# Moving key and softmax-weight transposes from TensorE to the SP DMA queue in an attention + FFT-gate kernel

## The chip, the cores and the metric

The kernel runs on one core of one Trainium2 chip. The metric is device time of one launch in microseconds (us); lower is better. A profile is one launch seen by the hardware profiler; its span is about 2 us shorter than the launch. Executions come in a fast and, at times, a slower state with a lower granted TensorE clock; verdicts use fast runs. Engines: PE is TensorE, PEld its weight loads, DVE VectorE, ACT ScalarE, POOL GpSimd, SP the SyncE queue that issues DMAs (SPq in the tables). An instruction that issues a DMA holds SP for a time; the next one in the queue can only start after it. A DMA lands when its data has arrived.

## The reference, cut to what matters

```python
# q, k, v: (8, 8, 576, 64); p: (8, 8, 32, 64)
p_packed = sm_attn(p, k, v)              # 32 packed queries read 576 keys
out = sm_attn(q, p_packed, p_packed)     # 576 queries read the 32 packed ones
x = out.transpose(0, 2, 1, 3).reshape(8, 576, 512)
proj = x @ w_proj                        # three blocks x1, x2, x3
y = x1 * irfft(rfft(x2) * rfft(filter)) * x3
return y @ w_out
```

## The kernel before: what the change and the argument touch

All is in fp16 on TensorE with fp32 sums. The kernel treats batches 0 to 7 as a pipeline of four stages: `front` (both attentions), `turn` (projection, first part of the spectrum, transposed softmax weights), `middle` (spectrum and gate) and `back` (inverse and output product). A helper records every operation and then plans the order of each engine with a cost model of its own, which takes 60 ns for issuing a DMA on SP and keeps the best of eight plans. All operations therefore carry one source line, L440, and any edit can move instructions far from it.

Three operands must be turned so that the contracted index lies on the partitions: queries `qT`, keys `kT`, and the normalised softmax weights `a2t`. Queries of batches 4 to 7 are turned by DMA on SP already:

```python
TURNED = 4
...
if b >= TURNED:                                   # in load(b)
    nc.sync.dma_start_transpose(qT.rearrange("p h i c -> p (h i) c"),
                                qn.rearrange("p h x -> p (h x)"))
```

Keys and weights are turned on PE, into a PSUM tile that DVE or ACT copies to SBUF:

```python
def k_turn(g):                                    # in front(b), four groups a batch
    tp = pst(f"kTp_b{b}", [P, 2, 3, KP], FP16)
    for hh in range(2):
        for ii in range(3):
            nc.tensor.transpose(tp[:, hh, ii, :], kn[:, 2 * g + hh, ts(ii, P)], ident[0:KP, 0:KP])
    ...                                           # copy on DVE or ACT
...
for t in range(2):                                # in turn(b)
    tp = pst(f"a2tp_b{b}", [P, S], FP16)
    nc.tensor.transpose(tp[:, ds(COL0[4] - 64 * t, P)], a2c, ident[:])
    for i in range(4):
        to = tp[:, ds(COL0[i], P)] if i != 2 else ...   # column order of the spectrum
        nc.tensor.transpose(to, a2n[:, i, ts(t, P)], ident[:])
    nc.vector.tensor_copy(out=a2t[:, t, :], in_=tp[:])
```

SP issues in its own order, and the stores of the outputs go through it too, from five buffers `os`.

The softmax here doesn't subtract the row's maximum and nothing guards it: scores larger than these inputs give would overflow.

## Time and profile before

| before | value |
|---|---|
| time, median of 3 runs | 201.28 us (200.71 to 203.0) |
| span of the profiled run | 198.3 us at a mean clock of 0.992 |
| PE busy from 131.4 to 190 us | 57.97 of 58.60 us |
| PE transposes: keys, weights | 192 of 96x96, 80 of 128x128 |

PE is the bound: the prediction below shows the busy lines, the chain and the stretches. A stretch line is read as its window in us, its length, then busy time with the number of instructions for PE, PEld, DVE, ACT and POOL, then the granted clock (1.00 is full), the DMA share and GB/s.

### The profile page before, as it was taken

Reading aid. Unit: us, or ns where it says so; the run is one execution under the profiler, and the core shown is the slowest. Engines: PE = TensorE matmul, PEld = TensorE weight load, DVE = VectorE, ACT = ScalarE, POOL = GpSimd, SP = SyncE. Lnnn points to the kernel's source line nnn. Section 1 sums busy time; section 2 is a strip of 40 time slices with the busy share of each in tenths; the row PEclk is TensorE's granted clock in tenths of the full one; section 3 lists DMA queues with packets and bytes.
Section 4 is the critical chain, followed back from the end, with each engine's and each line's share of the span. In section 5 each row is a group of like instructions: output and inputs, shape, how many; then the busy total and the mean of one; then the engine's idle time right before and its main releaser. Section 6 shows DMA issues by size and latency. Waiting matters only on the chain.

```text
span 198.3 us, 5799 instructions
## 1 busy us (share of the span) xinstructions
PE 184.8 (93%) x2413; PEld 114.7 (58%) x2413; DVE 142.2 (72%) x268; ACT 126.4 (64%) x265; POOL 133.5 (67%) x108
## 2 busy tenths in 40 slices
PE   4879989989999999999999999999999999999990
PEld 2226555666765775766665666565756465664630
DVE  4246857998369699966896699668966996798610
ACT  2247567597879978758874878478758556416050
POOL 7404578878566699989966996299529985963100
PEclk9999999999999999999999999999999999999996
DMA  5999999999999999889999999943013103503235
GB/s 136 270 269 197 205 207 198 196 199 195 202 217 268 189 201 179 165 116 244 263 173 156 112 126 201 172 130 85 3 55 107 56 0 118 143 10 132 81 126 141
DMA packets 44843, 30.96 MB, mean 156 GB/s; under 512 B 16336, under 2 KB 39376, under 8 KB 44816
## 3 DMA queue, kind: packets, MB, share of 16 engines
q0 software_dynamic: 29312, 16.52, 60.9%
q1 hardware_dynamic: 14784, 13.34, 28.9%
q10 hardware_dynamic: 720, 0.72, 1.2%
q8 instruction: 19, 0.31, 0.6%
q14 instruction: 8, 0.07, 0.1%
HBM read 35.55 MB, written 9.44 MB: 227 GB/s over the span
## 4 chain that ended last, share of the span: by engine, by line
PE 73%; DVE 8%; DMA 7%; POOL 4%; ACT 3%; issue 1%; ACTq 0%; DVEq 0%; POOLq 0%
PE x_b L440 28%; PE o_b L440 14%; PE f_b L440 7%; DMA kn_b<-in_k_dram 7%; PE fp_b L440 5%; PE s_b L440 4%; DVE tt_b L440 3%; PE kTp_b L440 3%; PE pv_b L440 3%; PE qp_b L440 3%; PE hp L440 2%; DVE zs_b L440 2%; PE a2tp_b L440 2%; PE qTp_b L440 1%; POOL gm_b L440 1%; POOL fa_b L440 1%
## 5 line engine op out<-in xcount | busy, mean ns | idle before, releaser
L440 POOL TENSOR_TENSOR gm_b<-tt_b,tt_b 128x512 f16<-128x512 f32 (+1 forms) x28 | 39.3, 1431 | 5.8 <-DVE tt_b L440 5.3
L440 DVE TENSOR_TENSOR tt_b<-f_b,h 128x1024 f32<-128x1024 f32 x32 | 38.7, 1214 | 4.7 <-PE f_b L440 4.1
L440 PE MATMUL x_b<-a2t_b,qm_b 128*128 128x512 f16 (+1 forms) x256 | 40.9, 286 | 0.2
L440 PE MATMUL x_b<-ac,gm_b 128*128 128x64 f16 (+3 forms) x312 | 36.0, 252 | 0.1
L440 ACT ACTIVATE os_b<-o_b 128x512 f32<-128x512 f32 x36 | 21.4, 597 | 21.8 <-PE o_b L440 21.8
L440 PE MATMUL o_b<-wout,y_b 128*128 128x512 f16 x128 | 33.4, 379 | 0.0
L440 ACT CAST qm_b<-qp_b 128x512 f16<-128x512 f32 x48 | 26.6, 590 | 10.6 <-PE qp_b L440 10.5
L440 POOL TENSOR_TENSOR tt_b<-tt_b,tt_b 128x1024 f32<-128x1024 f32 x12 | 28.3, 2360 | 5.0 <-DVE tt_b L440 4.9
L440 DVE TENSOR_TENSOR w_b<-x1s_b,x_b 128x512 f32<-128x512 f32 (+1 forms) x40 | 24.6, 627 | 8.9 <-ACT x1s_b L440 8.7
L440 ACT COPY x1s_b<-x_b 128x512 f32<-128x512 f32 (+1 forms) x40 | 21.9, 547 | 11.1 <-PE x_b L440 7.7
L440 PEld LDWEIGHTS <-gm_b 128*128 128x128 f16 x312 | 22.3, 98 | 8.8 <-POOL gm_b L440 2.6
L440 POOL TENSOR_TENSOR fa_b<-ez_b 128x512 f16<-128x512 f32 x14 | 17.6, 1273 | 14.2 <-ACT ez_b L440 14.2
L440 PE MATMUL f_b<-qm_b,fa_b 128*128 128x512 f16 x80 | 24.1, 379 | 0.4 <-DVE tt_b L440 0.2
L440 ACT ACTIVATE e_b<-s_b 96x384 f16<-96x384 f32 (+1 forms) x48 | 23.5, 533 | 1.1 <-PE s_b L440 1.0
L440 DVE SCALAR_TENSOR_TENSOR y_b<-w_b,x_b 128x512 f16<-128x512 f32 x32 | 20.6, 681 | 3.9 <-PE x_b L440 3.7
L440 PEld LDWEIGHTS <-a_b 128*128 128x128 f16 x240 | 15.9, 98 | 8.5 <-POOL a_b L440 1.2
L440 PEld LDWEIGHTS <-qm_b 128*128 128x128 f16 x256 | 15.7, 98 | 8.6 <-issue 1.1
L440 POOL TENSOR_TENSOR a_b<-e_b,zr_b 128x1152 f16<-128x1152 f16 (+2 forms) x10 | 17.3, 1735 | 3.5 <-ACT qm_b L440 2.4
L440 PEld LDWEIGHTS <-y_b 128*128 128x128 f16 x128 | 11.9, 98 | 11.5 <-DVE y_b L440 0.6
L440 PE MATMUL kTp_b<-ident,kn_b 96*128 96x96 f16 x192 | 13.0, 205 | 0.9 <-DVE tt_b L440 0.5
L440 PEld LDWEIGHTS <-kn_b 96*128 96x128 f16 x192 | 11.0, 97 | 4.7 <-issue 2.0
L440 ACT COPY ez_b<-fp_b 128x512 f32<-128x512 f32 x16 | 9.4, 586 | 3.7 <-PE fp_b L440 3.4
(78 smaller groups left out, 280.4 us busy)
## 6 DMA issues: line engine op xcount, KB each, us to landing
out_dram<-os_b SPq DMA_DIRECT2D x24, 256.0 KB, 2.7
kn_b<-in_k_dram POOLq DMA_DIRECT2D x8, 576.0 KB, 13.1
vn_b<-in_v_dram POOLq DMA_DIRECT2D x8, 576.0 KB, 14.8
qn_b<-in_q_dram POOLq DMA_DIRECT2D x8, 512.0 KB, 15.1
out_dram<-os_b SPq DMA_DIRECT2D x16, 128.0 KB, 2.4
wp<-in_moe_w_proj_dram POOLq DMA_DIRECT2D x3, 512.0 KB, 18.5
filt<-in_moe_filter_fft_dram SPq DMA_DIRECT2D x4, 256.0 KB, 6.6
out_dram<-os_b SPq DMA_DIRECT2D x16, 64.0 KB, 1.9
```

Of the source, the lines that this page charges most:

```text
L440: ins = op.call(*op.args, **op.kw).ins
```

## The change

The intent is to take PE time out of the stretches where PE is full. Keys of batches 6 and 7 (four DMAs of 144 KB a batch) and softmax weights of batches 5 to 7 (twelve DMAs a batch, six of 128 rows and 128 columns and six of 64 rows) are turned on SP. Queries of batches 4 to 7 stay as they were.

```diff
--- before.py
+++ after.py
@@ -506,7 +506,8 @@
 
     pflat = p.rearrange("b h j d -> (b h j) d").rearrange("(b t r) d -> r b t d", t=2, r=P)
 
-    TURNED = 4
+
+    TURNED, TURNED_K, TURNED_A = 4, 6, 5
 
 
     loaded, small = {}, {}
@@ -664,20 +665,27 @@
                 nc.vector.tensor_copy(out=qTm[:, :, u, c].rearrange("p g (e r) -> p g e r", e=2),
                                       in_=tp[:, :, c].rearrange("p g (r e) -> p g e r", e=2))
 
-        k_turn(0)
-        yield 260
+        for g in range(4) if b >= TURNED_K else ():
+            nc.sync.dma_start_transpose(kTr[g][:, 0:6 * KP].rearrange("p (x r) -> p x r", r=KP),
+                                        kn[:, 2 * g:2 * g + 2, :].rearrange("p h x -> p (h x)"))
+        if b < TURNED_K:
+            k_turn(0)
+            yield 260
         pack()
         yield 230
-        k_turn(1)
-        yield 260
+        if b < TURNED_K:
+            k_turn(1)
+            yield 260
         score1(0)
         yield 270
-        k_turn(2)
-        yield 260
+        if b < TURNED_K:
+            k_turn(2)
+            yield 260
         score1(1)
         yield 270
-        k_turn(3)
-        yield 260
+        if b < TURNED_K:
+            k_turn(3)
+            yield 260
         score1(2)
         yield 270
         if b < TURNED:
@@ -807,7 +815,12 @@
         nc.scalar.copy(out=fa[:, :, 512:640].rearrange("p t (u f) -> p t u f", u=2),
                        in_=fp[:].unsqueeze(2).broadcast_to([P, 2, 2, 64]))
         yield 300
-        for t in range(2):
+        for t in range(2) if b >= TURNED_A else ():
+            for i in range(4):
+                for r, c in ((slice(0, P), COL0[i]),) if i != 2 else ((slice(0, 64), 320), (slice(64, P), MAIN)):
+                    nc.sync.dma_start_transpose(a2t[:, t, c:c + r.stop - r.start], a2n[r, i, ts(t, P)])
+            nc.sync.dma_start_transpose(a2t[:, t, ds(COL0[4], 64)], a2c[64 * t:64 * t + 64, :])
+        for t in range(2) if b < TURNED_A else ():
             tp = pst(f"a2tp_b{b}", [P, S], FP16)
 
             nc.tensor.transpose(tp[:, ds(COL0[4] - 64 * t, P)], a2c, ident[:])
```

## The prediction

> **What bounds the kernel now.** I read the page first, then the busy times in stretches that follow the kernel's own rhythm, then the waits, and then the timeline around the work that the change takes away. The page says that TensorE (PE) is busy almost throughout at a granted clock that the slices print as 9 in all but the last one, and that no other engine is close:
>
> ```profile
> PE 184.8 (93%) x2413; PEld 114.7 (58%) x2413; DVE 142.2 (72%) x268; ACT 126.4 (64%) x265; POOL 133.5 (67%) x108
> ...
> PE 73%; DVE 8%; DMA 7%; POOL 4%; ACT 3%; issue 1%; ACTq 0%; DVEq 0%; POOLq 0%
> ```
>
> One batch passes every 20.7 us in the steady part: the first key transposes of successive batches start at 114.7 and 135.3 us. Cut into such periods, and the last two stretches without attention work, the columns are PE, weight loads, DVE, ACT, POOL busy, granted clock, DMA share, GB/s:
>
> ```profile
> 90.00:110.70 20.70, 20.55 (x292) 13.08 (x289) 16.07 (x29) 14.99 (x34) 17.00 (x14) 1.00 1.24 203
> 110.70:131.40 20.70, 20.61 (x297) 13.27 (x295) 16.54 (x30) 15.31 (x34) 15.23 (x10) 1.00 1.11 149
> 131.40:152.10 20.70, 20.23 (x286) 12.96 (x284) 16.16 (x30) 14.74 (x33) 14.22 (x10) 1.00 0.23 68
> 152.10:170.00 17.90, 17.74 (x165) 10.05 (x163) 14.94 (x24) 10.83 (x22) 14.70 (x10) 1.00 0.23 69
> 170.00:188.00 18.00, 18.00 (x146) 10.61 (x144) 14.05 (x21) 5.76 (x11) 9.09 (x6) 1.00 0.29 89
> ```
>
> PE is full in each (20.55 of 20.70, 18.00 of 18.00), DVE has 4 us to spare in a period and POOL 3 to 6. So PE's own stream sets the time from about 80 us to 188 us, and PE time taken out there should come off the end. The DMA column matters too: the engines are full (above 1.0, because packets of two queues overlap) until the last loads land at about 123 us, and nearly idle afterwards.
>
> **What the skill says.** (1) "VectorE: DVE Perf Modes", section "The three transpose paths", gives 390 ns for a 128x128 transpose on TensorE and 1309 ns by DMA. In this trace PE pipelines them: six key transposes hold the stream 0.31 us and five weight transposes 0.25 us (below), so 390 ns would overstate the gain seven times. (2) "DMA: Bandwidth & Descriptors", section "Anatomy of one DMA", puts about 2 us of fixed cost on each transfer, mostly the receipt. The trace agrees: the 64 KB output stores late in the run land 1.7 us after issue (median), the 256 KB ones 2.1. (3) The same page, "Issuing engines are not separate DMA queues", says that all queues share the same 16 engines and interleave. The trace shows how hard this bites: the four query transposes already there move 512 KB each, and their issue and landing depend on what else runs:
>
> ```profile
> L440 SPq DMA_TRANSPOSE qT_b<-qn_b x4: 1937/5840/10869, 73.7 to 112.8; - x4
> ...
> DMA to landing us min/median/max: 4.3/10.9/18.1
> ...
> 79.41 1.94 SPq L440 DMA_TRANSPOSE qT_b<-qn_b  x1
> ...
> 102.86 6.79 SPq L440 DMA_TRANSPOSE qT_b<-qn_b  x1
> ...
> 112.78 10.87 SPq L440 DMA_TRANSPOSE qT_b<-qn_b  x1
> ```
>
> Alone on the engines (79.4 us) one held SP for 1.94 us and landed in 4.3; beside the loads of the next batch it held SP for 6.8 and 10.9 us, and the one of 102.86 landed 18.1 us later. (4) "Advanced Engine Details and Errata", section "X-Bar Transpose (TRN2)", calls them as fast as ordinary DMAs; that holds here for the lone case at best.
>
> **The change, part by part.** Removed from PE: for batches 6 and 7 four groups of six 96x96 key transposes, for batches 5 to 7 two groups of five weight transposes. The weight-load stream shows what each group costs, as the distance to the next load behind it:
>
> ```profile
> 141.25 0.37 PEld L440 LDWEIGHTS <-kn_b 96*128 96x128 f16 x6
> 141.56 0.36 PEld L440 LDWEIGHTS <-qm_b 128*128 128x128 f16 x3
> ...
> 151.43 0.29 PEld L440 LDWEIGHTS <-a_b 128*128 128x128 f16 x5
> 151.68 0.15 PEld L440 LDWEIGHTS <-y_b 128*128 128x128 f16 x2
> ```
>
> Keys: 4 x 0.31 = 1.25 us a batch, two batches 2.5 us. Weights: 2 x about 0.27 = 0.54 us a batch, three batches 1.6 us. Sum 4.1 us of PE, all after about 114 us, where PE is full. Also removed: eight copies of kT (0.45 us on DVE, 0.64 on ACT, four each) and six of a2t (0.45 us on DVE), 7.1 us of two engines that don't bound, so worth nothing directly; and their PSUM tiles.
>
> Added on SP: 8 key pieces of 144 KB, and 36 small weight transposes (12 a batch). SP is in order, the built program gives it eight completion semaphores in turn, and each issue waits for the transfer eight before it. For a small one I estimate 0.45 to 0.5 us of SP: a plain store held it 0.33 to 0.59, and the lone 512 KB transpose, sixteen blocks, 1.94, so about 0.1 per block on top. Twelve take 6 us, plus some 2.3 us to land: 8 to 8.5 us from weights to transposed weights.
>
> Is each in time? In the instruction order of the changed program the weights of batch 6 are ready, by the old trace's times, some 15 us before their first gate, and those of batch 7 are ready at 160.3 (end of the POOL normalisation) with the first gate at about 171: 10.7 us once the PE transposes are out of the way, against 8.4. Both are hidden, the second with 2 us to spare. Those of batch 5 sit behind the query and key transposes of batch 7 on SP, and come out about where PE wants them (I get 135 us for both), so 0 to 1 us of wait. Keys of batch 7 fall after 123 us, with idle DMA engines, and have several us to spare.
>
> The keys of batch 6 are the weak place. On SP they come straight behind the query transpose of batch 6, between 97 and 120 us, where the loads of batch 7 run. The old trace moved the 2048 packets of that query transpose at roughly 170 a us beside the loads and near 1000 alone. Queries and keys of batch 6 are now 2048 + 2304 packets. The changed order loads the queries of batch 6 earlier (the value load of batch 5 moves ahead), so SP can start near 96 rather than 102.86; at a mixed rate the last piece lands between 114 and 124 us. PE wants the first piece at about 116.5 and the fourth at about 119. Taking the landing as even over 113 to 125, the mean wait is 6/12 x 3 = 1.5 us, with up to 5 possible.
>
> One more loss: key transposes now fill PE while it waits for the gated spectra from POOL:
>
> ```profile
> PEld L440 <- POOL gm_b L440: 2.2, 6, 0.5
> ```
>
> That is over 114 to 160 us. With filler gone the wait may grow by some tenths; I set 0.3 us for this and for batch 5's weights together.
>
> Sum: 201.28 - 4.1 + 1.5 + 0.3 = 199.0 us.
>
> **Rivals.** (a) Everything is hidden and the whole 4.1 us comes off: 197.2. For it: PE is at 18.00 of 18.00 in the tail, batch 7 has slack, DMA is nearly idle after 123. Against it: the mixed DMA rates just shown. (b) The keys of batch 6 come 4 to 5 us late. PE runs in order, so this undoes the gain, and delays what SP holds behind them: 200.5 to 202. For it: the 18.1 us landing. Against it: the earlier query load. (c) SP becomes the bound through output stores queued behind transposes, as the five output buffers fill and ACT, then PSUM, then PE stop. In the changed order at most four or five outputs stand behind a block of transposes, just what the buffers hold, so I give this little; it would cost 2 to 4 us, 201 to 203. (d) The kernel plans its order anew, and the plan differs from the start of the program, where nothing was edited (other order of the filter products, 32 fillers for 35). That moves the time by perhaps 1 us either way and can't be foreseen from the profile.
>
> **Range and chances.** The full gain is 2.0% of 201.28, so over 2% faster needs nearly all of it kept and some luck with the new plan or with the keys: 0.20. Slower by over 2% (205.3) needs (b) and (c) together: 0.07. Rest 0.73. Range 196.4 (full gain and 0.8 us of luck) to 202.0 (rival b).
>
> **What would show it.** Right: in the changed profile PE's key transposes count 144 instead of 192 and the weight ones 50 instead of 80, PE's waits from 110 us on are mainly for kT of batch 6 (1 to 2 us in all) and little for a2t; the small transposes hold SP about 0.5 us each; the period between batches falls from 20.7 to about 19. Wrong: a wait of over 3 us at the score products of batch 6; a2t waits of over 1 us for batch 6 or 7 (then the small transposes cost SP much more than 0.5 us); ACT waiting for output buffers; or a difference that is already there at 80 us, which would be the new plan and not the transposes.

## The result, and the profile after

The changed kernel takes 219.22 us (median of 4 runs, 215.86 to 221.16); the kernel before took 201.0 us (199.9 to 203.0) beside it. Ratios here are the mean time of one kernel's fast runs over that of the other's in the same rounds, so not quite the ratio of the quoted medians: 1.083, with a 95% interval of 1.064 to 1.102. The change makes the kernel 8% slower, and the prediction of 199.0 us with a range up to 202.0 is wrong.

The page of the profile after, its busy line, its clock line (one digit for each of 40 slices, 9 is full speed) and the chain of work that ended last:

```profile
PE 186.7 (87%) x2332; PEld 112.4 (53%) x2332; DVE 139.1 (65%) x258; ACT 124.5 (58%) x261; POOL 133.4 (62%) x108
...
PEclk9999999999999999999999999975799889999999
...
PE 53%; SPq 20%; DMA 12%; DVE 6%; ACT 3%; issue 2%; POOL 2%; ACTq 0%; DVEq 0%
```

PE has 81 instructions fewer than before (2332 for 2413: 78 transposes and 3 of the `spin` matmuls that fill idle time) and is yet busy for longer; its clock sinks in slices 27 to 29, 32 and 33. The SP queue, which had no part in the chain before, now makes up 20% of it. The three late stretches, same windows as in the prediction but for the last, which ends at 190 (there PE was busy for all of 170 to 190 us before):

```profile
131.40:152.10 20.70, 13.14 (x123) 7.23 (x120) 7.46 (x12) 9.72 (x21) 11.86 (x8) 0.75 0.37 61
152.10:170.00 17.90, 16.07 (x214) 9.10 (x213) 13.24 (x22) 11.70 (x24) 12.44 (x9) 0.97 0.23 55
170.00:190.00 20.00, 18.17 (x138) 10.19 (x136) 12.87 (x19) 7.91 (x15) 12.71 (x8) 0.94 0.26 69
```

PE is idle for 20.70 - 13.14 = 7.6 us of the first, where it had been idle for 0.5, and for 11.2 us of all three. The DMA engines are mostly idle too (0.23 to 0.37), so it isn't bandwidth. What does SP do meanwhile? Its timeline (start, us, instruction, count):

```profile
121.14 4.90 SPq L440 DMA_TRANSPOSE qT_b<-qn_b  x1
126.14 0.52 SPq L440 DMA_DIRECT2D out_dram<-os_b  x1
126.78 6.04 SPq L440 DMA_TRANSPOSE kT<-kn_b  x4
132.90 16.08 SPq L440 DMA_TRANSPOSE a2t_b<-a_b  x12
149.09 4.34 SPq L440 DMA_DIRECT2D out_dram<-os_b  x8
153.53 16.36 SPq L440 DMA_TRANSPOSE a2t_b<-a_b  x12
169.99 3.11 SPq L440 DMA_DIRECT2D out_dram<-os_b  x6
173.21 15.65 SPq L440 DMA_TRANSPOSE a2t_b<-a_b  x12
```

From 132.90 to 188.9 us SP is free for 0.11 us at most between two instructions, but for one gap of 0.46 us. Twelve small transposes keep it for 15.7 to 16.4 us, not 6. A store holds it for 4.34 / 8 = 0.54 us. The group of the weight transposes (minimum, median and maximum hold in ns) and its landing:

```profile
L440 SPq DMA_TRANSPOSE a2t_b<-a_b x36: 1093/1226/1828, 132.9 to 187.6; - x36
...
DMA to landing us min/median/max: 2.2/2.4/3.9
```

The median hold is 1.23 us. From the start of its first transpose to the landing of its last a batch needs 16.8 to 17.5 us (the landing counts from the issue, so the last hold is in it), where the prediction counted 8 to 8.5 and had 10.7. What PE then waits for, in its timeline (idle time before the piece in brackets):

```profile
121.11 0.26 PE L440 MATMUL s_b<-pk,kT 128*128 128x64 f16 x3 [1.63 <-DMA kT<-kn_b]
123.15 0.35 PE L440 MATMUL s_b<-pk,kT 128*128 128x64 f16 x6 [0.82 <-DMA kT<-kn_b]
...
140.99 0.38 PE L440 MATMUL x_b<-a2t_b,qm_b 128*128 128x512 f16 x1 [1.50 <-DMA a2t_b<-a_b]
...
147.71 1.44 PE L440 MATMUL x_b<-a2t_b,qm_b 128*128 128x512 f16 x3 [5.86 <-DMA a2t_b<-a_b]
...
187.63 0.81 PE L440 MATMUL x_b<-a2t_b,qm_b 128*128 128x512 f16 x3 [1.83 <-DMA a2t_b<-a_b]
```

The list of waits sums them up (us, times, longest):

```profile
PE x_b L440 <- DMA a2t_b<-a_b: 9.2, 3, 5.9
...
PEld L440 <- DMA kT<-kn_b: 3.0, 3, 1.8
PE s_b L440 <- DMA kT<-kn_b: 2.4, 2, 1.6
```

PEld runs beside PE, so the last two rows are largely one wait, of about 3 us. A fourth wait of PE for the weights stands under `issue`: 1.83 us up to 168.58, when a weight transpose of batch 6 had just landed (168.49).

The clock adds to it. Its records give half speed from 141.78 to 152.02 us, a stretch that begins with the 5.86 us wait (141.86 us), just after two shorter ones (0.20 and 1.50 us), and from 169.08 to 172.50, after the wait that ended at 168.58. PE is busy for 4.38 and 3.42 us of these; at full speed about half of that would have done (an estimate), so they cost some 3.9 us.

Where the time comes from is easiest to see at fixed points of the program. The kernel makes 36 output products; every fourth of them, from the first on, is a fixed point, nine in all. The table gives their starts in the profiled runs (us):

| | 1st | 4th | 5th | 6th | 7th | 8th | 9th |
|---|---|---|---|---|---|---|---|
| before | 50.8 | 111.3 | 131.0 | 149.0 | 165.8 | 178.8 | 189.3 |
| after | 52.3 | 113.5 | 134.9 | 161.5 | 180.3 | 194.7 | 205.3 |
| difference | +1.5 | +2.2 | +3.9 | +12.5 | +14.5 | +15.9 | +16.0 |

The working: +2.2 us by the 4th point, which is there at the 2nd already (83.5 and 85.6 us), while SP issues the first moved transpose at 107.44 us; +1.7 to the 5th (the wait of 3.0 for keys of batch 6, less the 1.25 of PE work taken away); then 11.2 - 0.6 = 10.6 us more PE idle time, + 3.9 for the clock, - 2.9 for the other PE work taken away (1.6 for weights, 1.25 for keys of batch 7). After 190 us PE has no idle time up to the 9th point in either run. The sum is 15.5 us; the spans differ by 214.0 - 198.3 = 15.7.

### The profile page after: what moved, and what is told of

It is laid out like the page before. It is cut to its first block, busy times and chain, and to the rows that moved or that the text cites.

```text
span 214.0 us, 5700 instructions
## 1 busy us (share of the span) xinstructions
PE 186.7 (87%) x2332; PEld 112.4 (53%) x2332; DVE 139.1 (65%) x258; ACT 124.5 (58%) x261; POOL 133.4 (62%) x108
## 4 chain that ended last, share of the span: by engine, by line
PE 53%; SPq 20%; DMA 12%; DVE 6%; ACT 3%; issue 2%; POOL 2%; ACTq 0%; DVEq 0%
SPq L440 20%; PE x_b L440 18%; PE o_b L440 8%; DMA kT<-kn_b 6%; PE hp L440 4%; PE f_b L440 4%; PE fp_b L440 4%; PE s_b L440 4%; DMA filt<-in_moe_filter_fft_dram 3%; DVE tt_b L440 2%; DMA a2t_b<-a_b 2%; PE pv_b L440 2%; PE qp_b L440 2%; PE kTp_b L440 2%; PE qTp_b L440 2%
## 5 line engine op out<-in xcount | busy, mean ns | idle before, releaser
L440 PE MATMUL x_b<-a2t_b,qm_b 128*128 128x512 f16 (+1 forms) x256 | 42.2, 291 | 11.4 <-DMA a2t_b<-a_b 9.2
L440 PE MATMUL x_b<-ac,gm_b 128*128 128x64 f16 (+3 forms) x312 | 38.2, 260 | 0.4 <-ACT qm_b L440 0.4
L440 POOL TENSOR_TENSOR tt_b<-tt_b,tt_b 128x1024 f32<-128x1024 f32 x12 | 28.3, 2358 | 16.1 <-DVE rz_b L440 15.1
L440 PE MATMUL o_b<-wout,y_b 128*128 128x512 f16 x128 | 33.9, 379 | 0.0
L440 PEld LDWEIGHTS <-gm_b 128*128 128x128 f16 x312 | 23.3, 100 | 10.6 <-issue 2.3
L440 POOL TENSOR_TENSOR fa_b<-ez_b 128x512 f16<-128x512 f32 x14 | 17.6, 1271 | 13.6 <-ACT ez_b L440 13.6
L440 PEld LDWEIGHTS <-a_b 128*128 128x128 f16 x210 | 13.9, 98 | 8.4 <-POOL a_b L440 1.5
L440 PE MATMUL s_b<-pk,kT 128*128 128x64 f16 x192 | 11.3, 198 | 2.4 <-DMA kT<-kn_b 2.4
L440 PEld LDWEIGHTS <-kT 128*128 128x128 f16 x192 | 9.3, 101 | 6.4 <-DMA kT<-kn_b 3.0
```

Of the source, the lines that this page charges most:

```text
L440: ins = op.call(*op.args, **op.kw).ins
```

## The experiments

The theory, called H below, is: a transpose DMA holds SP for about 1.23 us however small it is, so the number of instructions, not the bytes, makes the weights late, and all else on SP with them. Its rivals: the keys of batch 6 are the main loss; the planner misjudges SP (it takes 60 ns for the hold); the new plan is worse from the start on, where nothing was edited. The before kernel was run beside each group, at medians of 200.3 to 201.6 us. All fourteen kernels gave correct results.

### e1: the keys alone

```diff
-    TURNED, TURNED_K, TURNED_A = 4, 6, 5
+    TURNED, TURNED_K, TURNED_A = 4, 6, 8
```

> Weights go back to TensorE, keys of batches 6 and 7 stay on the DMA. Theory H (hold): every transpose instruction, however small, holds the SP queue about 1.23 us (36 of 36 weight transposes in the changed profile took 1.09 to 1.83 us), so twelve a batch make a 15 us serial chain that PE, and the stores behind it, wait for. Then all of the loss goes with the weights: 199 to 202 us, with a wait of PE for kT of batch 6 of 3 to 6 us left. Rival K (keys): the keys of batch 6, landing 12 us after issue beside the loads, are what costs: stays at 212 us or more. Rival P (plan): the new order of the whole kernel is worse: also over 205, as the plan changes here too.

Measured: 205.87 us (15 runs, 202.36 to 207.47, many of them slow), ratio of fast runs 1.011 (1.007 to 1.016). In the profiled run the fixed points are 2.8 us late at the first and 2.5 at the last. All of that loss is there at the 2nd fixed point (+3.4 us), before the first moved transpose; of what comes after, keys of batch 6 take about 1.3 us (a wait of 2.4 us for `kT` in the weight loads, less 1.25 of work) and those of batch 7 give it back. The time is a little above what H allowed, but some 14 us of the 16 are not the keys.

### e2: the weights alone

```diff
-    TURNED, TURNED_K, TURNED_A = 4, 6, 5
+    TURNED, TURNED_K, TURNED_A = 4, 8, 5
```

> Keys go back to TensorE, weights of batches 5 to 7 stay on the DMA in twelve pieces each. H: the 15 us chain of twelve transposes is all still there, three times: 213 to 219 us, PE waiting for a2t 8 us or more in all. K: 198 to 202 us.

Measured: 211.28 us (4 runs, 206.27 to 213.72). Only the profiled run, 206.27, was fast, so there is no ratio. The fixed points go from -0.9 to +6.4 us: the weights alone cost 7.3 us, less than H expected. PE waits 7.5 us for `a2t`. Why less than in the full change? The SP timeline:

```profile
121.08 16.92 SPq L440 DMA_TRANSPOSE a2t_b<-a_b  x12
...
144.04 15.73 SPq L440 DMA_TRANSPOSE a2t_b<-a_b  x12
```

Those of batch 5 begin at 121.08 us instead of 132.90, where they stood behind the query and key transposes of batch 7, and cost PE only 0.60 us; those of batches 6 and 7 cost it 4.33 and 2.58 us. So the two halves of the change do not add: keys alone cost nothing after the start, weights alone 7.3 us, both together 14.5 (from +1.5 to +16.0). They share one queue.

### e3: the full change with seven weight transposes a batch

The same bytes; an instruction takes both halves `t` where the layout allows it (`a2c` twice).

```diff
-        for t in range(2) if b >= TURNED_A else ():
-            ... twelve transposes of one block or 64 rows
+        if b >= TURNED_A:
+            for i in (1, 3, 0):
+                nc.sync.dma_start_transpose(a2t[:, :, ds(COL0[i], P)], a2n[:, i, :])
+            for r, c in ((slice(0, 64), 320), (slice(64, P), MAIN)):
+                nc.sync.dma_start_transpose(a2t[:, :, ds(c, 64)], a2n[r, 2, :])
+            for t in range(2):
+                nc.sync.dma_start_transpose(a2t[:, t, ds(COL0[4], 64)], a2c[64 * t:64 * t + 64, :])
```

> The whole change, but the same bytes of the weights by seven instructions a batch instead of twelve (both halves t of one source tile in one instruction). H: the hold goes by the instruction: 7 x 1.23 = 8.6 us a batch instead of 15.2, each of the chains of batches 6 and 7 gets 6.6 us shorter: 203 to 208 us. If instead the hold goes by bytes or packets moved (rival B), each of the double ones holds SP about 2.4 us and the time stays at 214 to 220.

Measured: 204.46 us (203.52 to 205.97), ratio 1.020 (1.010 to 1.030), slower than before, but by more or less than 2% is unclear. The SP timeline:

```profile
133.12 9.85 SPq L440 DMA_TRANSPOSE a2t_b<-a_b  x7
...
147.84 10.06 SPq L440 DMA_TRANSPOSE a2t_b<-a_b  x7
```

The median hold is still 1.24 us, with twice the bytes in five of the seven, and PE waits only 1.5 us for `a2t`. With the number of instructions alone, three quarters of the loss went (8.3% to 2.0%). The fixed points are 3.5 us late at the 4th and 3.7 at the last: what remains is lost before the moved transposes (+3.5 at the 2nd).

### e5: two transposes a batch into a staging tile

```diff
+            nc.sync.dma_start_transpose(a8[:, 0:8, :], a2[:, 0:4 * HJ])
+            nc.sync.dma_start_transpose(a8[:, 8, :], a2c)
+            # cut: five nc.vector.tensor_copy calls bring the blocks into a2t's columns
```

> The whole change, but the weights by two transposes a batch (one of 128x1024, one of 128x128) into a staging tile, and four small copies on DVE that put the columns in order. H: SP is held under 3 us a batch, PE no longer waits for a2t: 198 to 202 us, the keys of batch 6 still costing 3 to 6 us of wait. B: the big one holds SP 8 x 1.2 = 10 us, 210 us or more.

Measured: 212.61 us (211.39 to 215.51), ratio 1.056 (1.046 to 1.066): a miss. The profile is of a run in the slow state (215.51). The eight-block transposes held SP 1.26 to 1.29 us each (once 2.69), as H has it, but the copies now stand in DVE's order, and DVE waits with them. DVE's timeline:

```profile
140.04 4.46 DVE L440 COPY a2t_b<-a_b 128x512 f16<-128x512 f16 x4 [3.90 <-DMA a_b<-a_b]
```

SP reached batch 5's transpose at 135.39 us only, behind the query and keys of batch 7; DVE stood still for 3.90 us, and PE waited 5.7 us for the product `w` that DVE had to make next. The clock records again show 10.24 us at half speed. The late landing came in through another engine.

### e4: the full change, with a planner that knows the hold

The diff shows one of the two places where the planner takes the time.

```diff
-            return 760 if self.engine == "POOL" else 60, 4000 + self.transfer_ns()
+            return self.hold_ns(), 4000 + self.transfer_ns()   # transposes 1270, other DMAs on SP 450
```

> The whole change, same instructions, but the kernel's own planner is told that a transpose holds SP 1.27 us and any other DMA 0.45 us, where it took 0.06 for both. H with misplanning: the planner now sees the chain of twelve and puts other PE work ahead of the first gates: 203 to 209 us, the a2t waits of PE cut by half or more. H without it (nothing to put there, the chain is simply too long): 213 us or more.

Measured: 219.31 us (218.2 to 220.29), ratio 1.094 (1.087 to 1.100). Knowing the hold does not help: the work on SP is too long, not only badly placed. The waits show the output stores behind the transposes as well (the helper's line is L446 here, as the edit adds lines above it):

```profile
ACT os_b L446 <- DMA out_dram<-os_b: 10.7, 5, 5.8
...
PE x_b L446 <- ACT os_b L446: 8.3, 2, 5.4
```

That is rival (c) of the prediction, in this kernel and not in the changed one.

### e6 and e7: the keys of batch 7 alone, and weights of batches 6 and 7 in seven pieces

```diff
+    TURNED, TURNED_K, TURNED_A = 4, 7, 8      # e6
+    TURNED, TURNED_K, TURNED_A = 4, 8, 6      # e7, with the seven transposes of e3
```

> Keys of batch 7 alone on the DMA, weights all on TensorE. Keys-only of batches 6 and 7 was 1.1% slower, with PE waiting some 4 us for the keys of batch 6, whose transposes run beside the loads. If that wait was the reason, this one has no wait for kT and gains the 1.25 us of PE: 199.0 to 201 us, ratio 0.990 to 1.0. If it is the new plan or SP's outputs behind the transposes, it stays at 1.01.

> Weights of batches 6 and 7 alone on the DMA, seven instructions a batch; keys on TensorE. SP has no other transposes then. H: the chain of 8.6 us and 2.3 us to land just fits: PE waits under 1.5 us for a2t, gain of two times 0.54 us of PE against it: 199.5 to 202 us. If twelve instructions were not the problem but weights by DMA as such, 205 us or more.

Measured: e6 199.84 us (20 runs), ratio 0.994 (0.991 to 0.997), with no wait for `kT`; e7 199.86 us (20 runs), ratio 0.995 (0.991 to 0.998), with no wait for `a2t`. The gains are 0.6% and 0.5%; the prediction's PE times for these parts, 1.25 and 2 x 0.54 us, are 0.6% and 0.5% of 201. Both are small, but neither interval reaches 1. So the gain was sized rightly where the transfers are in time.

### e8: the hold by itself

The kernel before, with eight transposes of other sizes from batch 7's weights into a tile that nobody reads any more.

```diff
+            for rows, blocks in ((P, 1), (64, 1), (16, 1), (P, 2), (P, 4), (P, 8), (P, 1), (P, 8)):
+                ... nc.sync.dma_start_transpose(spare[...], a2[...])
```

> The kernel before, with eight further transposes late on SP, from the weights of batch 7 into a query buffer that nobody reads any more: 128x128, 64x128, 16x128, and 2, 4, 8 blocks of 128x128 in one instruction, one and eight once more. H: the hold goes by the instruction: 1.2 us for 16 rows as for 128, under 1.4 us for eight blocks. B: it goes by rows: 0.2 us for 16 rows and 9 us for eight blocks. Time as before, 200 to 203 us, as PE waits for none of them.

Measured: one run of 206.45 us. SP's timeline, single instructions in the order of the list (128 rows, 16 rows, 2, 4, 8 blocks):

```profile
166.75 1.13 SPq L440 DMA_TRANSPOSE qT_b<-a_b  x1
...
173.44 1.08 SPq L440 DMA_TRANSPOSE qT_b<-a_b  x1
...
176.92 1.25 SPq L440 DMA_TRANSPOSE qT_b<-a_b  x1
...
179.53 1.92 SPq L440 DMA_TRANSPOSE qT_b<-a_b  x1
183.12 1.23 SPq L440 DMA_TRANSPOSE qT_b<-a_b  x1
```

Sixteen rows hold it for 1.08 us, eight blocks, 64 times the bytes, for 1.23 and 1.33. The 1.92 at four blocks is an odd one: holds of about 1.8 us occur now and then at other sizes (1.83 and 1.75 among the weights of the changed kernel), and the five eight-block transposes of e5 and e11 held SP for 1.26, 1.29, 1.58, 2.00 and 2.69 us. The time misses what was expected, for a reason away from the probe: the records have half clock from 15.3 to 28.9 us, the first fixed point is 6.4 us late and so is the last. The start shows what happened: PE waited 2.16 us for the converted filter at 13.77 us, and half clock followed; PE was busy for 13.37 us of that stretch, and half of it, 6.7 us (an estimate), covers the 6.4 us. Its late part is as before, so the eight holds cost nothing there.

### e10, e11 and e12: both parts that were in time, a staged form, and twelve pieces

```diff
+    TURNED, TURNED_K, TURNED_A = 4, 7, 6      # e10, seven transposes; e11, staged as in e5
+    TURNED, TURNED_K, TURNED_A = 4, 8, 6      # e12, the twelve of the change
```

> Keys of batch 7 and weights of batches 6 and 7 (seven instructions a batch) on the DMA, nothing of batch 6's keys or batch 5's weights. The two parts alone measured 0.9939 and 0.9947 of before. If they add up as PE time: ratio 0.986 to 0.992, about 198.3 to 199.5 us. If SP's queue now has too much again, as in the seven-instruction version of the whole change: 1.0 or more.

> As the run with keys of batch 7 and weights of 6 and 7, but the weights by two transposes a batch into a staging tile, and copies on DVE. In the staged version of the whole change DVE stood in order behind weights of batch 5 that SP reached late, and PE waited for DVE. Without batch 5: SP holds 2.5 us a batch, no DVE wait over 1 us, 198 to 200.5 us. If the copies on DVE are themselves the trouble: over 203 us.

> Weights of batches 6 and 7 only, in the change's own twelve pieces a batch; same bytes and same batches as the run with seven instructions (0.9947 of before). H: 15.2 us of SP a batch instead of 8.6, against some 11 us between weights and first gate: PE waits for a2t 3 to 8 us in all, 203 to 208 us. If the number of instructions does not matter: 199 to 201 us.

Measured: e10 199.42 us (6 runs, 196.57 to 201.42) against 200.33 before, ratio 0.989 (0.983 to 0.994); e11 199.68 us (12 runs), 0.994 (0.991 to 0.998); e12 206.07 us (4 runs, 201.81 to 209.9, the profiled one slow, no ratio). e12 differs from e7 in the number of instructions alone: batch 6's hold SP for 16.22 us instead of 9.83, and PE waits 3.7 us for `a2t` where e7 has no wait. With one fast run in four, its time itself can't be compared. e10 beats both kernels, by 1.1% the kernel before: the sum of e6 and e7. Its late stretches:

```profile
131.40:152.10 20.70, 20.59 (x286) 12.37 (x290) 17.49 (x31) 14.71 (x33) 16.10 (x12) 1.00 0.39 111
152.10:170.00 17.90, 17.90 (x155) 10.22 (x140) 13.35 (x20) 10.46 (x20) 15.45 (x11) 1.00 0.26 73
```

PE is full again at full clock. Staging gains nothing over seven direct pieces.

### e13: the keys of batch 6 alone

```diff
-        for g in range(4) if b >= TURNED_K else ():
+        for g in range(4) if b == TURNED_K else ():     # and b != TURNED_K for the PE transposes; TURNED_A = 8
```

> Keys of batch 6 alone on the DMA (four pieces), everything else of the change undone. Batch 7's keys alone measured 0.9939 of before and both together 1.0113. If batch 6's keys are what makes the difference: PE waits 3 to 5 us for kT and the ratio is 1.01 to 1.02 (202.5 to 205 us). If the two interact on SP's queue instead: no such wait, ratio 0.99 to 1.0.

Measured: 205.12 us (4 runs), ratio 1.014 (1.001 to 1.027); the profile, slow, has PE wait 3.5 us for `kT` and its weight loads 4.0, and the fixed points go from +2.8 at the 4th to +7.1 at the 5th; 3.4 us at half speed follow the wait. These keys are a loss by themselves, beside the loads of batch 7, but a small one.

### e14 and e16: is the start to blame on the order of the filter loads?

In the changed kernel's plan SP loads the filter's rows in another order. Here only plans with the old order are taken; e14 is e1 and e16 the full change.

```diff
-            if best is None or end < best[0]:
+            start = [o.n for o in order if o.dma() and o.engine == "SP"][:7]
+            if start == sorted(start) and (best is None or end < best[0]):
```

> Keys of batches 6 and 7 only, as in the keys-only run (1.0113 of before), but the planner may only choose among its plans with the filter loads in the old order. If the start made the loss: the first output product comes at about 51 us again (before 50.8, keys-only 53.6) and the ratio is 0.990 to 1.0. If PE's wait for the keys of batch 6 made it: first output product at 51 us and the ratio still 1.005 to 1.015.

> The whole change, with the filter loads in the old order by the same choice among plans. The weights theory puts all but some 2 to 3 us of the loss after 125 us: 213 to 218 us, ratio 1.06 to 1.085. If the start were the larger part, 205 us or less.

Measured: e14 204.9 us, ratio 1.014 (1.002 to 1.025); e16 220.14 us, 1.092 (1.081 to 1.102). The start did not come back: the first fixed point is at 54.5 and 55.9 us, later than in e1 and the changed kernel. Both profiles are of slow runs, but the fast ratios did not fall either. This doesn't clear the order of the loads, because these two runs lose their start in another way.

The clock records show how. The first filter products follow each other at 0.43 us, and at 0.22 us once full speed is recorded; the kernel before reaches it at 10.81 us. In the changed kernel, e1, e3, e5 and e13, which all move keys of batch 6, PE stands for 2.3 to 4.1 us from about 8 us on, in wait for filter data, and full speed comes at 15.5 to 17.4 us. In e14 and e16 it is there at 6.95 and 8.77 us, but two waits of 1.4 to 1.9 us for converted filter data follow, and half speed from 13.78 to 20.60 and from 15.60 to 22.42 us. So the start is late by waits for the filter and by the half clock around them. Why the plans bring these waits stays open.

## Why the prediction was wrong

**The step that failed** is "For a small one I estimate 0.45 to 0.5 us of SP", and with it "Twelve take 6 us, plus some 2.3 us to land: 8 to 8.5 us from weights to transposed weights". I drew a line through a store (0.33 to 0.59 us) and one sixteen-block transpose (1.94 us). The runs show that the two do not lie on one line: 1.08 us at 16 rows, 1.23 at eight blocks, so nearly all of it is a fixed hold of the instruction. Twelve take 15.7 to 16.4 us, more than the 10.7 us there were for batch 7. e3 against the full change shows it with the bytes unchanged, and so do the holds and waits of e12 against e7. The prediction had named the sign: PE waited 1.83 us for `a2t` of batch 6 and as much for batch 7, over its 1 us. The page "VectorE: DVE Perf Modes" of the Trainium skill, section "The three transpose paths", stood in my working with its 1309 ns for one 128x128 transpose by DMA. It is within 7% of the measured hold of 1226 ns, and I used it for nothing but the comparison with PE. It doesn't say that SP is held for that time; an estimate with it would have been 12 x 1.31 = 15.7 us, more than the 10.7 us for batch 7. The reading of the trace in (4) was wrong as well: "holds here for the lone case at best" had no ordinary DMA beside it. Query loads of the same 512 KB took 15.1 us to land (median of the kernel before), the four query transposes 10.9.

**Keys of batch 6** were "the weak place" as predicted, by the mechanism predicted: the chain after has the transfer on its path.

```profile
110.40 12.70 DMA kT<-kn_b
```

The mis-sized term is "the mean wait is 6/12 x 3 = 1.5 us": it was 3.0 us in the changed kernel, 2.4 in e1 and 4.0 in e13.

**"0.3 us for this and for batch 5's weights together"** failed for the same reason as the first step, and more: batch 5's transposes started at 132.90, near the 135 us that I had for their coming out, and PE waited 1.50 + 5.86 us for them. In e2, where they start 12 us earlier, 0.60 us of that wait is left.

**The gain of 4.1 us** was right where it could be tested: e6, e7 and e10 give 0.6, 0.5 and 1.1%, and PE's transposes count 144 and 50 after, as predicted.

**Rivals.** (a) fell. (b) came with its smaller half: in e1 the late keys of batch 6 undo the gain of both batches' keys, not more. In e13, a slow profile, they cost 4.3 us between the 4th and 5th point, half speed included. (c) does not show in the changed kernel, where no engine waits long for output buffers, but it does in e4. (d) is real and larger than "perhaps 1 us either way": without any edit there, the first fixed point lay from 2.0 us earlier (e4) to 6.4 later (e8), and in the latter, as in e14, the clock was at half speed for part of the start. The full change's own start was +1.5 to +2.2 us. The waits for the filter and the clock make it (see e14); why the plan brings them is not settled.

**What I missed altogether** is the clock: a bound engine that has to wait for some microseconds comes back slower. The page "TensorE: Matmul & The Clock Gate" of the Trainium skill, section "HAM oscillation — how this bites in real kernels", puts it as "no PE-idle gaps >~3.4µs", after which TensorE is throttled to half. I had not drawn on it. The trace agrees: in the changed kernel and in e5 a wait of 5.86 and 5.7 us goes with 10.24 us at half speed. So a late transfer should have been priced with its aftermath. No run here takes the wait away and nothing else, so the cause rests on the page and on their coming together.

The traces of all sixteen kernels show more than I had read from them: it need not be one long gap. Each of the 17 switches to half speed between the start and 190 us came after 3.41 us in which PE was busy for 1.71 us or less, in one wait or several; the stretches last 3.41 us or two, three or four times that, and full speed came back after 3.41 us with PE busy for at least 3.23. Two other such periods at full speed (1.55 and 1.64 us busy) had no switch after them, so this describes these traces and is no exact rule.

## What to carry to other kernels

Count the instructions on an in-order DMA queue, not their bytes: on SP here a transpose costs about 1.2 us of the queue for anything from 16 rows to eight blocks, with some holds up to 2.7 (and key pieces beside loads up to 4.0), so pack blocks into one instruction, and check the whole queue (transposes, stores and whatever waits behind) against the time between a producer and its first reader. Move only what has slack: the same idea with keys of batch 7 and seven pieces for the weights of batches 6 and 7 gains 1.1%, while all of it loses 8%. When no profile row has your instruction at your size, don't interpolate from another kind; time one by itself first.

## What the Trainium skill lacked or had wrong

- "VectorE: DVE Perf Modes", section "The three transpose paths": it has 1309 ns for a 128x128 transpose by DMA but not that the issuing queue is held for nearly this time and that the hold hardly depends on the size (other pages give sequencer time per transpose only in a part on trn3). Measured: 1.23 us median of 36, 1.08 us for 16 rows, 1.23 to 1.58 for five of seven with eight blocks (the others 2.00 and 2.69). Its 390 ns on TensorE is not what one costs in a stream: about 0.05 us each here (0.31 us for six, 0.25 for five).
- "DMA: Bandwidth & Descriptors", section "Issuing engines are not separate DMA queues": it calls the sequencer's time to initiate a DMA "usually small relative to the DMA itself". For these transposes it was 1.23 us against 2.4 us to landing, and SP was taken up for 56 us almost without a break.
- "Advanced Engine Details and Errata", section "X-Bar Transpose (TRN2)": "as fast as regular DMAs" fits the landing here (small transposes 2.4 us, output stores 2.5 to 2.8, medians in the changed kernel) but leaves out the issuing side: a transpose held SP for 1.23 us, a store for 0.54.
- "TensorE: Matmul & The Clock Gate", section "HAM oscillation — how this bites in real kernels": its gap of about 3.4 us is not the least that shows half speed; 3.41 us with PE busy for half of the time or less went before every switch here. In the changed kernel a pause of 1.83 us, ending at 168.58 us, was followed by half speed from 169.08 to 172.50; in the probe e8 one of 2.16 us, with shorter ones around it, was followed by 13.6 us of half speed.
